# Attention and a dense layer on one core: deeper buffers for the weights' conversion, and the first scores sent in two halves

## The chip, the core and the metric

The kernel runs on one core of a Trainium2 chip. The core has TensorE (matrix products, in the profile PE, its weight loads PEld), VectorE (DVE), ScalarE (ACT), GpSimd (POOL) and SyncE (SP, which here only issues DMAs); they run side by side and wait for one another by semaphores. The time is the device time of one execution in microseconds (us); lower is better. Three runs of the kernel before gave a median of 971.5 us (971.06 to 972.27).

## What is computed

Talking-heads attention over 4 batches, 12 heads, 448 positions and 64 channels, then a gated dense layer over its 1792 rows:

```python
scores = scale * np.matmul(q, k.transpose(0, 1, 3, 2))
scores = np.einsum('bhij,hg->bgij', scores, w_pre)      # mix over heads
attn = softmax(scores)
attn = np.einsum('bhij,hg->bgij', attn, w_post)         # mix over heads again
x = np.matmul(attn, v)                                  # then rows (b, s), columns (h, d): 1792 x 768
h = x @ w_in                                            # w_in 768 x 2048
out = (h * (1 / (1 + np.exp(-h)))) @ w_out              # w_out 2048 x 768
```

The two dense weights come as 64-bit floats and have to be turned into 32-bit ones on the chip.

## The kernel before

**Attention.** Each batch's 448 queries are cut into 4 tiles of 12 or 11 groups of 10 queries, 180 groups in 16 tiles. For a tile, TensorE makes scores head by head (line 277), ScalarE and VectorE copy them to SBUF (`st`, or `first` for tile 0, lines 282 and 284) and a DMA regroups them (line 286): `g` has one partition for each pair of query and head, so that one product mixes the heads. For each group, `mix` (315) multiplies with w_pre, `top` (321) takes the maximum on VectorE, `exp` runs on ScalarE (326), `norm` makes 1/sum on VectorE (331, 332) and scales w_post by it on GpSimd (`wr`, 334), `mix_again` (341) multiplies with it, ScalarE copies the result (`at`, 349). `values` (297) multiplies with v.

**The opening.** Before the loop, tile 0's keys and queries are transposed (`prep_k`, `prep_q`) and its scores made; `banks` and `steps` set the order. All of tile 0's score regrouping has to be in `g` before its first mix. The first four heads of tile 1's scores come here too.

**The loop** (from line 546) takes one group at a time: the mix of group i+3, copies, the maximum, `norm` of i+2, the exp of i+3, then scores, transposes and values that a table `work` gave to this group, then `mix_again` of i. Each engine runs its instructions in the order written.

**The weights' conversion** (`convert`, line 38) is a generator that the loop steps along. A weight block (a job) is two parts; a part takes two groups of the loop. It loads 256 KB into a buffer `cw` (47), VectorE takes the exponent (88), ScalarE shifts it (92), VectorE puts sign and mantissa in (94, 95) and, one part later, joins the low word (64), GpSimd multiplies (67). After two parts GpSimd makes sums (70 to 73) into `ct` and into the block `cg`, and two stores send both to DRAM (57, 58). 42 of 48 jobs run in attention, in the groups of the set `lighter` (which holds every group of the loop up to the last tile); the other 6 run in the dense layers. Buffers: three `cw`, two `cg`, one `ct`. At part k the load of part k+1 is issued:

```python
        if k > 1:
            load(k + 1)
```

into the buffer that part k-2 gave back. A tile's buffers belong to a pool; an instruction that writes one first waits for everything that used it before.

**DMA queues.** Nearly every DMA is issued by SyncE, in the order of the program. A DMA that waits for its data, or for the DMA eight places earlier to land, holds up those behind it.

**After attention** the converted blocks are loaded (`wl`, 485), split in high and low parts and multiplied (501 to 503).

Of the kernel before, what the change touches and what calls it, by code (L numbers as in the profile page):

```python
# [8 lines left out]
F32 = mybir.dt.float32  # L9
F32R = mybir.dt.float32r  # L10
I32 = mybir.dt.int32
# [11 lines left out]
def raw(ap):  # L23

    return ap.bitcast(F32)
# [9 lines left out]
    eng.tensor_sub(out=lo, in0=x, in1=raw(hi))  # L35


def convert(nc, pool, ebias, jobs):

    parts = [(n, i) for n in range(len(jobs)) for i in (1, 0)]  # L40
    loaded, made = [], []

    def load(k):
        if k < len(parts):
            n, i = parts[k]
            ws = pool.tile([128, 2, 256], I32, name="cw", tag="cw", bufs=3)
            nc.sync.dma_start(out=ws, in_=jobs[n][0][:, i])
            loaded.append(ws.rearrange("p q (w t) -> p q w t", t=2))

    for k in range(3):  # L50
        load(k)
    yield

    def store():
        while made:
            dst, g, t = made.pop(0)
            nc.sync.dma_start(out=dst[:, :4], in_=g)
            nc.sync.dma_start(out=dst[:, 4:], in_=t)

    def finish(k, pair, g, e):  # L60
        n, i = parts[k]
        lo, hi = pair[:, :, :, 0], pair[:, :, :, 1]
        m = lo.bitcast(F32)
        nc.vector.scalar_tensor_tensor(  # L64
            out=m, in0=lo.bitcast(U32), scalar=(1 if i else -1) * 2.0 ** -32, in1=hi,
            op0=ALU.mult, op1=ALU.add if i else ALU.subtract)
        nc.gpsimd.tensor_mul(out=e, in0=m, in1=e)  # L67
        if not i:
            t = pool.tile([128, 3, 128], F32, name="ct", tag="ct", bufs=1)
            nc.gpsimd.tensor_add(out=t[:, 0], in0=g[:, 0], in1=g[:, 1])  # L70
            nc.gpsimd.tensor_add(out=t[:, 1], in0=g[:, 0], in1=g[:, 2])
            nc.gpsimd.tensor_add(out=t[:, 2], in0=t[:, 0], in1=g[:, 2])
            nc.gpsimd.tensor_add(out=g[:, 0], in0=t[:, 2], in1=g[:, 3])
            made.append((jobs[n][1], g, t))

    before = None
    for k in range(len(parts)):
        if k > 1:
            load(k + 1)
        pair = loaded.pop(0)  # L80
        hi = pair[:, :, :, 1]
        if k % 2 == 0:
            g = pool.tile([128, 4, 128], F32, name="cg", tag="cg", bufs=2)
        else:
            store()
        half = g[:, 2 * (k % 2):2 * (k % 2) + 2]
        e = half.bitcast(I32)
        nc.vector.tensor_scalar(out=e, in0=hi, scalar1=0x7FF00000, scalar2=None, op0=ALU.bitwise_and)  # L88
        if before:
            finish(*before)  # L90
        yield True
        nc.scalar.activation(out=e, in_=e, func=AF.Relu, scale=8.0, bias=ebias)  # L92
        yield False
        nc.vector.scalar_tensor_tensor(out=e, in0=hi, scalar=-2 ** 31, in1=e, op0=ALU.bitwise_and, op1=ALU.bitwise_or)
        nc.vector.tensor_scalar(out=hi, in0=hi, scalar1=0xFFFFF, scalar2=1 << WEXP, op0=ALU.bitwise_and, op1=ALU.bitwise_or)
        before = k, pair, g, half
        yield
    if before:
        finish(*before)
    yield  # L100
    store()
    yield
# [3 lines left out]
def talking_heads_then_silu_mlp(  # L106
# [11 lines left out]
    nc = tc.nc  # L118
# [4 lines left out]
    R = 10  # L123
# [114 lines left out]
    def load_q(n, hg, queue=nc.sync):  # L238
        b, ti = seq[n]
        t0, m, _ = tiles[ti]  # L240
        qns[n, hg] = nat.tile([TQ, HH, D], F32, name="qn", tag="qn", bufs=2)
        queue.dma_start(out=qns[n, hg][:m], in_=q[b, hg * HH:(hg + 1) * HH, t0:t0 + m, :].rearrange("h p d -> p h d"))

    def prep_q(n, hg):

        t0, m, ng = tiles[seq[n][1]]
        NP = HH // 2
        qh, ql = qs[n, hg] = [q2_p.tile([128, NP, TQ], F32R, name=x, tag=f"{x}{hg}") for x in ("qh", "ql")]
        qn = qns.pop((n, hg))
        pt = bank(banks[0], "pt")  # L250
        for hh in range(NP):
            nc.tensor.transpose(
                pt[:, hh * m:(hh + 1) * m], qn[:m, 2 * hh:2 * hh + 2, :].rearrange("p h d -> p (h d)"), ident[:m, :m])
        src = pt[:, :NP * m].rearrange("p (h g i) -> p h g i", h=NP, i=R)
        hi, lo = (x[:, :, :m].rearrange("p h (i g) -> p h g i", i=R) for x in (qh, ql))

        def take_high():
            nc.scalar.copy(out=hi, in_=src)

        def take_low():  # L260
            nc.vector.tensor_sub(out=lo, in0=src, in1=raw(hi))
        return [(take_high, take_low)]

    def scores(n, h):

        b, ti = seq[n]
        t0, m, ng = tiles[ti]
        if h == 0:
            gs[n] = g_ps[(len(seq) - 1 - n) % 2].tile([GP, 12, S], F32, name="g", tag="g")
        qh, ql = qs[n, h // HH]  # L270
        kh, kl = ks[b, h]
        hh = h % HH // 2
        ps = [bank(banks[0], "pqk") for _ in range(2)]
        for step, (q_, k_) in enumerate(((qh, kh), (ql, kh), (qh, kl))):
            for i in range(2):
                rows = slice(i * D, (i + 1) * D)
                nc.tensor.matmul(ps[i][:m, :S], lhsT=q_[rows, hh, :m], rhs=k_[rows], start=(step == 0), stop=(step == 2))  # L277

        def take(i):
            st = s_p.tile([TQ, S], F32, name="st", tag="s") if n else first_scores[:, h + i]  # L280
            if i:
                nc.vector.tensor_copy(out=st[:m], in_=ps[i][:m, :S])  # L282
            else:
                nc.scalar.copy(out=st[:m], in_=ps[i][:m, :S])  # L284
            queue = nc.scalar if n == 0 and i == 0 and h % 4 == 2 else nc.sync
            queue.dma_start(out=gs[n][h + i:GP:H, :ng, :], in_=st[:m])
        return [(lambda: take(0), None), (None, lambda: take(1))]

    def values(n, h):
# [63 lines left out]
    jobs = [(wi_src[:, f, c], wi_dram[:, :, f * HC + c, :]) for f in range(HF) for c in range(HC)]  # L353
    jobs += [(wo_src[:, c, f], wo_dram[:, :, c * HF + f, :]) for c in range(HC) for f in range(HF)]
    NA = 42
    conv = convert(nc, c_p, ebias, jobs[:NA])

    groups, first = [], []
    for n, (b, ti) in enumerate(seq):
# [46 lines left out]
    lighter = set()  # L406
    for i in range(0, n_last, 10):
        lighter |= set(sorted(range(i, min(i + 10, n_last)), key=lambda i: weight[i - 1] if i else 0.0)[:10])
    lighter |= {n_last - 1, n_last - 2}


    first_scores = a_p.tile([TQ, H, S], F32, name="first", tag="at")
# [11 lines left out]
    steps += [(prep_q, 1, 0)] + [(scores, 1, 2 * h) for h in range(NE)]  # L424
    nk = 6
    weights = load_weights()
    for j, (what, *args) in enumerate(steps):
        banks[:] = [(ps_m, ps_m, ps_p, ps_a)[j % 4]]
        takes = what(*args)
        for take in (x for t in takes for x in t):  # L430
            if take:
                take()
        if what is prep_k and nk < H:
            load_k_pair(0, nk)
            nk += 2
        if j == 5:
            next(weights)
            load_q(1, 0, nc.gpsimd)
        if j == 12:
            load_q(1, 1, nc.gpsimd)  # L440
    banks[:] = [ps_m]
    for _ in weights:
        pass
    for i in range(3):
        at(i).mix()
        at(i).top()
# [337 lines left out]
```

## Time and profile before

| | us |
|---|---|
| median of three runs | 971.5 |
| the profiled execution | 972.25 |
| its span, first to last instruction | 970.5 |
| TensorE busy | 918.2 |
| VectorE busy | 635.6 |
| ScalarE busy | 543.4 |
| GpSimd busy | 453.4 |

An engine that is busy for a large share of the span isn't for that reason the limit at every moment: TensorE's matmuls are pipelined, their ends are modelled, and its busy time stretches where the clock is lower. The granted clock is the share of TensorE's full clock that was given in a stretch; 0.5 is the lower of its two levels. Who waits for whom is inferred from semaphores; an instruction that waits for several is put down to the one that came last.

### The profile page before, as it was taken

Reading aid. Unit: us, or ns where it says so; the run is one execution under the profiler, and the core shown is the slowest. Engines: PE = TensorE matmul, PEld = TensorE weight load, DVE = VectorE, ACT = ScalarE, POOL = GpSimd, SP = SyncE. Lnnn points to the kernel's source line nnn. Section 1 sums busy time; section 2 is a strip of 40 time slices with the busy share of each in tenths; the row PEclk is TensorE's granted clock in tenths of the full one; section 3 lists DMA queues with packets and bytes.
Section 4 is the critical chain, followed back from the end, with each engine's and each line's share of the span. In section 5 each row is a group of like instructions: output and inputs, shape, how many; then the busy total and the mean of one; then the engine's idle time right before and its main releaser. Section 6 shows DMA issues by size and latency. Waiting matters only on the chain.

```text
span 970.5 us, 18406 instructions
## 1 busy us (share of the span) xinstructions
PE 918.2 (95%) x6216; PEld 742.3 (76%) x6216; DVE 635.6 (65%) x1414; ACT 543.4 (56%) x1256; POOL 453.4 (47%) x627
## 2 busy tenths in 40 slices
PE   6789999999899989998999999999999999999997
PEld 4466676667676666665767999889999999889996
DVE  4577676657676757666665069865568977997432
ACT  4466676667576757666667455522368435443242
POOL 1154444444345434444444256895333767784130
PEclk9899999999999989999999999999999999999999
DMA  6677765767667768767563035521122113221134
GB/s 161 171 208 192 198 190 170 209 195 201 186 174 219 192 170 217 193 182 199 166 179 104 1 112 155 148 60 44 55 66 65 55 51 84 66 66 55 47 87 114
DMA packets 166399, 131.18 MB, mean 135 GB/s; under 512 B 50134, under 2 KB 155466, under 8 KB 166306
## 3 DMA queue, kind: packets, MB, share of 16 engines
q1 hardware_dynamic: 164300, 128.66, 48.1%
q10 hardware_dynamic: 1782, 0.99, 0.4%
q8 instruction: 50, 0.82, 0.4%
q0 software_dynamic: 224, 0.35, 0.2%
q14 instruction: 43, 0.35, 0.1%
HBM read 63.74 MB, written 27.53 MB: 94 GB/s over the span
## 4 chain that ended last, share of the span: by engine, by line
PE 66%; DMA 12%; DVE 8%; POOL 5%; issue 4%; ACT 3%; SPq 1%; ACTq 0%; POOLq 0%; DVEq 0%
PE ph L503 12%; PE ph L502 12%; PE ph L501 12%; PE pa L341 9%; PE pp L315 8%; PE po L297 6%; DMA wi_dram<-cg 4%; PE pqk L277 4%; DMA cw<-in_moe_w_out 3%; DVE nm L321 2%; DMA cw<-in_moe_w_in 2%; DVE st L282 2%; POOL wl L491 1%; DMA kn<-in_k 1%; POOL cg L67 1%
## 5 line engine op out<-in xcount | busy, mean ns | idle before, releaser
L341 PEld LDWEIGHTS pa<-wr,e 120*112 120x112 f32 x1440 | 165.4, 178 | 42.7 <-issue 26.4
L491 POOL TENSOR_TENSOR wl<-wl,wh 128x512 fp32r<-128x512 f32 x84 | 122.0, 1462 | 156.0 <-ACT wh L490 151.2
L341 PE MATMUL pa<-wr,e 120*112 120x120 f32 x1440 | 187.7, 274 | 1.6 <-POOL wr L334 0.8
L334 POOL TENSOR_SCALAR wr<-wpost,r 120x120 f32<-120x120 f32 x180 | 78.7, 438 | 215.7 <-DVE r L332 170.4
L315 PE MATMUL pp<-g,wpre 120*120 120x448 f32 x360 | 169.5, 554 | 8.8 <-DMA g<-st 5.1
L503 PE MATMUL ph<-op,wl 128*128 128x448 f32 x462 | 169.2, 366 | 1.6 <-POOL wl L491 1.6
L501 PE MATMUL ph<-op,wh 128*128 128x448 f32 x462 | 170.4, 369 | 0.0
L502 PE MATMUL ph<-op,wh 128*128 128x448 f32 x462 | 168.8, 365 | 0.0
L321 DVE TENSOR_REDUCE nm<-pp 120x1 f32<-120x448 f32 x180 | 111.5, 620 | 83.5 <-PE pp L315 82.7
L326 ACT ACTIVATE e<-pp,nm 120x448 f32<-120x448 f32 x180 | 114.7, 637 | 80.7 <-DVE r L331 47.2
L349 ACT COPY at<-pa 112x480 f32<-112x480 f32 x180 | 102.3, 568 | 48.2 <-PE pa L341 48.1
L67 POOL TENSOR_TENSOR cg<-cw,cg 128x256 f32<-128x256 f32 x96 | 72.4, 755 | 93.1 <-DVE cw L64 93.1
L297 PEld LDWEIGHTS po<-at,v 112*64 112x64 f32 x1536 | 77.0, 140 | 37.4 <-ACT st L284 11.1
L503 PEld LDWEIGHTS ph<-op,wl 128*128 128x128 f32 x462 | 86.8, 188 | 10.1 <-POOL wl L491 3.1
L297 PE MATMUL po<-at,v 112*64 112x110 f32 (+1 forms) x1536 | 87.1, 268 | 6.8 <-ACT st L284 6.7
L501 PEld LDWEIGHTS ph<-op,wh 128*128 128x128 f32 x462 | 86.8, 188 | 6.8
L502 PEld LDWEIGHTS ph<-op,wh 128*128 128x128 f32 x462 | 86.8, 188 | 6.6
L88 DVE TENSOR_SCALAR cg<-cw 128x256 int32<-128x256 int32 x96 | 32.0, 334 | 79.5 <-DMA cw<-in_moe_w_out 26.1
L490 ACT CAST wh<-wl 128x512 fp32r<-128x512 f32 x84 | 51.0, 618 | 46.9 <-DMA wl<-wo_dram 26.3
L92 ACT ACTIVATE cg<-cg,ebias 128x256 int32<-128x256 int32 x96 | 49.1, 512 | 41.3 <-DVE cg L88 41.3
L509 DVE TENSOR_TENSOR op<-x,op 128x448 fp32r<-128x448 f32 x54 | 46.2, 866 | 31.2 <-ACT op L507 17.7
L315 PEld LDWEIGHTS pp<-g,wpre 120*120 120x120 f32 x360 | 53.1, 187 | 13.7 <-ACT e L326 7.1
(107 smaller groups left out, 1612.5 us busy)
## 6 DMA issues: line engine op xcount, KB each, us to landing
g<-st SPq DMA_DIRECT2D x144, 192.5 KB
cw<-in_moe_w_in SPq DMA_DIRECT2D x48, 256.0 KB
cw<-in_moe_w_out SPq DMA_DIRECT2D x48, 256.0 KB
wl<-wi_dram SPq DMA_DIRECT2D x42, 256.0 KB
wl<-wo_dram SPq DMA_DIRECT2D x42, 256.0 KB
g<-st SPq DMA_DIRECT2D x36, 210.0 KB
wi_dram<-cg SPq DMA_DIRECT2D x24, 256.0 KB
wo_dram<-cg SPq DMA_DIRECT2D x24, 256.0 KB
```

What stands on the lines that cost most here:

```text
L67: nc.gpsimd.tensor_mul(out=e, in0=m, in1=e)
L297: nc.tensor.matmul(po[i * D:(i + 1) * D, c * m:(c + 1) * m], lhsT=vs[b, h + 2 * c][:, i, j, :], rhs=ats[n][:, j, h + 2 * c + i, :m], start ...
L315: nc.tensor.matmul(self.p[:GP, :S], lhsT=wpre.rearrange("p i g -> p (i g)"), rhs=gs[self.n][:, self.slot, :], start=True, stop=True)
L321: nc.vector.tensor_reduce(out=self.nm, in_=self.p[:GP, :S], axis=AX.X, op=ALU.max, negate=True)
L326: nc.scalar.activation(out=self.e, in_=self.p[:GP, :S], func=AF.Exp, bias=self.nm, scale=1.0, accum_out=self.s)
L334: nc.gpsimd.tensor_scalar(out=self.wr, in0=wpost.rearrange("p g i -> p (g i)"), scalar1=r, scalar2=1.0, op0=ALU.mult, op1=ALU.mult)
L341: nc.tensor.matmul(self.pa[:JT, j * GP:(j + 1) * GP], lhsT=self.e[:, j * JT:(j + 1) * JT], rhs=self.wr, start=True, stop=True)
L349: nc.scalar.copy(out=ats[self.n][:, :, :, o:o + R], in_=self.src)
L491: nc.gpsimd.tensor_sub(out=wl, in0=raw(wl), in1=raw(wh))
L501: nc.tensor.matmul(p[:, :T], lhsT=wh, rhs=x[:, 0], start=(n == 0), stop=False)
L502: nc.tensor.matmul(p[:, :T], lhsT=wh, rhs=x[:, 1], start=False, stop=False)
L503: nc.tensor.matmul(p[:, :T], lhsT=wl, rhs=x[:, 0], start=False, stop=(n == nk - 1))
```

## The change

The conversion gets five `cw` buffers, three `cg` buffers and, in attention, two `ct` buffers, and loads three parts ahead. It no longer runs in groups 0 to 2. Tile 0's scores are sent to `g` in two halves of its twelve groups: for each head a store of groups 0 to 5 when its scores are copied, and the twelve stores of groups 6 to 11 after the last head; all of them on SyncE, where three of the twelve were on ScalarE. For the halves to be one block of partitions each, the query conversion of tile 0 is written half by half. The weights of the head mix are prepared earlier, and tile 1's second query half is loaded by SyncE behind the 24 stores, no longer by GpSimd.

```diff
--- before.py
+++ after.py
@@ -35,7 +35,7 @@
     eng.tensor_sub(out=lo, in0=x, in1=raw(hi))
 
 
-def convert(nc, pool, ebias, jobs):
+def convert(nc, pool, ebias, jobs, cts=1):
 
     parts = [(n, i) for n in range(len(jobs)) for i in (1, 0)]
     loaded, made = [], []
@@ -43,7 +43,7 @@
     def load(k):
         if k < len(parts):
             n, i = parts[k]
-            ws = pool.tile([128, 2, 256], I32, name="cw", tag="cw", bufs=3)
+            ws = pool.tile([128, 2, 256], I32, name="cw", tag="cw", bufs=5)
             nc.sync.dma_start(out=ws, in_=jobs[n][0][:, i])
             loaded.append(ws.rearrange("p q (w t) -> p q w t", t=2))
 
@@ -66,7 +66,7 @@
             op0=ALU.mult, op1=ALU.add if i else ALU.subtract)
         nc.gpsimd.tensor_mul(out=e, in0=m, in1=e)
         if not i:
-            t = pool.tile([128, 3, 128], F32, name="ct", tag="ct", bufs=1)
+            t = pool.tile([128, 3, 128], F32, name="ct", tag="ct", bufs=cts)
             nc.gpsimd.tensor_add(out=t[:, 0], in0=g[:, 0], in1=g[:, 1])
             nc.gpsimd.tensor_add(out=t[:, 1], in0=g[:, 0], in1=g[:, 2])
             nc.gpsimd.tensor_add(out=t[:, 2], in0=t[:, 0], in1=g[:, 2])
@@ -75,12 +75,11 @@
 
     before = None
     for k in range(len(parts)):
-        if k > 1:
-            load(k + 1)
+        load(k + 3)
         pair = loaded.pop(0)
         hi = pair[:, :, :, 1]
         if k % 2 == 0:
-            g = pool.tile([128, 4, 128], F32, name="cg", tag="cg", bufs=2)
+            g = pool.tile([128, 4, 128], F32, name="cg", tag="cg", bufs=3)
         else:
             store()
         half = g[:, 2 * (k % 2):2 * (k % 2) + 2]
@@ -251,14 +250,19 @@
         for hh in range(NP):
             nc.tensor.transpose(
                 pt[:, hh * m:(hh + 1) * m], qn[:m, 2 * hh:2 * hh + 2, :].rearrange("p h d -> p (h d)"), ident[:m, :m])
-        src = pt[:, :NP * m].rearrange("p (h g i) -> p h g i", h=NP, i=R)
-        hi, lo = (x[:, :, :m].rearrange("p h (i g) -> p h g i", i=R) for x in (qh, ql))
+        src = pt[:, :NP * m].rearrange("p (h g) -> p h g", h=NP)
+        W = 1 if n else 2
+        blocks = [slice(w * m // W, (w + 1) * m // W) for w in range(W)]
+        srcs = [src[:, :, w].rearrange("p h (g i) -> p h g i", i=R) for w in blocks]
+        his, los = ([x[:, :, w].rearrange("p h (i g) -> p h g i", i=R) for w in blocks] for x in (qh, ql))
 
         def take_high():
-            nc.scalar.copy(out=hi, in_=src)
+            for hi, src in zip(his, srcs):
+                nc.scalar.copy(out=hi, in_=src)
 
         def take_low():
-            nc.vector.tensor_sub(out=lo, in0=src, in1=raw(hi))
+            for lo, src, hi in zip(los, srcs, his):
+                nc.vector.tensor_sub(out=lo, in0=src, in1=raw(hi))
         return [(take_high, take_low)]
 
     def scores(n, h):
@@ -282,8 +286,16 @@
                 nc.vector.tensor_copy(out=st[:m], in_=ps[i][:m, :S])
             else:
                 nc.scalar.copy(out=st[:m], in_=ps[i][:m, :S])
-            queue = nc.scalar if n == 0 and i == 0 and h % 4 == 2 else nc.sync
-            queue.dma_start(out=gs[n][h + i:GP:H, :ng, :], in_=st[:m])
+            if n == 0:
+                for w in range(2):
+                    def put_scores(w=w):
+                        nc.sync.dma_start(out=gs[n][h + i:GP:H, 6 * w:6 * w + 6, :], in_=st[60 * w:60 * w + 60])
+                    if w:
+                        second.append(put_scores)
+                    else:
+                        put_scores()
+            else:
+                nc.sync.dma_start(out=gs[n][h + i:GP:H, :ng, :], in_=st[:m])
         return [(lambda: take(0), None), (None, lambda: take(1))]
 
     def values(n, h):
@@ -353,7 +365,7 @@
     jobs = [(wi_src[:, f, c], wi_dram[:, :, f * HC + c, :]) for f in range(HF) for c in range(HC)]
     jobs += [(wo_src[:, c, f], wo_dram[:, :, c * HF + f, :]) for c in range(HC) for f in range(HF)]
     NA = 42
-    conv = convert(nc, c_p, ebias, jobs[:NA])
+    conv = convert(nc, c_p, ebias, jobs[:NA], 2)
 
     groups, first = [], []
     for n, (b, ti) in enumerate(seq):
@@ -406,7 +418,7 @@
     lighter = set()
     for i in range(0, n_last, 10):
         lighter |= set(sorted(range(i, min(i + 10, n_last)), key=lambda i: weight[i - 1] if i else 0.0)[:10])
-    lighter |= {n_last - 1, n_last - 2}
+    lighter = lighter - set(range(3)) | {n_last - 1, n_last - 2}
 
 
     first_scores = a_p.tile([TQ, H, S], F32, name="first", tag="at")
@@ -424,6 +436,8 @@
     steps += [(prep_q, 1, 0)] + [(scores, 1, 2 * h) for h in range(NE)]
     nk = 6
     weights = load_weights()
+    next(weights)
+    second = []
     for j, (what, *args) in enumerate(steps):
         banks[:] = [(ps_m, ps_m, ps_p, ps_a)[j % 4]]
         takes = what(*args)
@@ -433,14 +447,15 @@
         if what is prep_k and nk < H:
             load_k_pair(0, nk)
             nk += 2
-        if j == 5:
-            next(weights)
+        if j == 3:
+            for _ in weights:
+                pass
             load_q(1, 0, nc.gpsimd)
-        if j == 12:
-            load_q(1, 1, nc.gpsimd)
+        if (what, *args) == (scores, 0, H - 2):
+            for put_scores in second:
+                put_scores()
+            load_q(1, 1)
     banks[:] = [ps_m]
-    for _ in weights:
-        pass
     for i in range(3):
         at(i).mix()
         at(i).top()
```

What SyncE issues in the opening, before. `qn` is a query half, `kn` a head's keys, `g<-first` tile 0's regrouping, `g<-st` tile 1's, `cw` the conversion's loads, `v` values:

```order
L242 DMA qn<-in_q 120x6x64
L214 DMA kn<-in_k 112x4x64 x6
L286 DMA g<-first 10x12x448 x9
L286 DMA g<-st 10x11x448 x4
L47 DMA cw<-in_moe_w_in 128x2x256 x3
L218 DMA v_384<-in_v 112x2x256
L218 DMA v_386<-in_v 112x2x256
```

And in the changed kernel, same place:

```order
L241 DMA qn<-in_q 120x6x64
L213 DMA kn<-in_k 112x4x64 x6
L292 DMA g<-first 10x6x448 x24
L241 DMA qn<-in_q 110x6x64
L298 DMA g<-st 10x11x448 x4
L47 DMA cw<-in_moe_w_in 128x2x256 x3
L217 DMA v_400<-in_v 112x2x256
L217 DMA v_402<-in_v 112x2x256
```

Nine whole stores became 24 halves, and a query load of tile 1 stands behind them.

What TensorE does from the first mix on, with its waits, in the changed kernel (`pp` is the mix, `pt` a transpose, `pa` the second mix; DMAHW0 to 7 are the eight semaphores that SyncE's and ScalarE's DMAs take in turn):

```order
L327 MATMUL pp<-g,wpre 120x448 [waits DMAHW4_49,DMAHW3_49,DMAHW5_49,DMAHW2_49,DMAHW6_49,DMAHW1_49,DMAHW7_49,DMAHW0_49,PE_49]
L327 MATMUL pp<-g,wpre 120x448 [waits PE_49]
L327 MATMUL pp<-g,wpre 120x448 [waits Activation_49] x2
L251 MATMUL pt<-ident,qn 128x110 [waits DMAHW6_49]
L251 MATMUL pt<-ident,qn 128x110 x2
L353 MATMUL pa<-wr,e 112x120 [waits Pool_49]
L353 MATMUL pa<-wr,e 112x120 x3
```

TensorE's own order is that of before; the transpose `pt` waited for GpSimd's queue there and now waits for SyncE's load. The mix of group 6 has waits on these semaphores of its own.

VectorE at the start of the last tile, before (`nm` is a group's maximum, `r` its 1/sum, `cg` and `cw` the conversion):

```order
L88 TENSOR_SCALAR cg<-cw 128x256
L64 SCALAR_TENSOR_TENSOR cw<-cw 128x256
L321 TENSOR_REDUCE nm<-pp 120x1
L331 TENSOR_SCALAR r<-s 120x1
L332 RECIPROCAL r<-r 120x1
L94 SCALAR_TENSOR_TENSOR cg<-cw,cg 128x256
L95 TENSOR_SCALAR cw<-cw 128x256
L321 TENSOR_REDUCE nm<-pp 120x1
L331 TENSOR_SCALAR r<-s 120x1
L332 RECIPROCAL r<-r 120x1
L64 SCALAR_TENSOR_TENSOR cw<-cw 128x256
L321 TENSOR_REDUCE nm<-pp 120x1
```

And in the changed kernel:

```order
L93 SCALAR_TENSOR_TENSOR cg<-cw,cg 128x256
L94 TENSOR_SCALAR cw<-cw 128x256
L87 TENSOR_SCALAR cg<-cw 128x256
L64 SCALAR_TENSOR_TENSOR cw<-cw 128x256
L93 SCALAR_TENSOR_TENSOR cg<-cw,cg 128x256
L94 TENSOR_SCALAR cw<-cw 128x256
L64 SCALAR_TENSOR_TENSOR cw<-cw 128x256
L333 TENSOR_REDUCE nm<-pp 120x1
```

The conversion's last part was spread between the groups' maxima and now stands in one block ahead of one.

## Rows read from the trace of the kernel before

**Rows 1.** The page: its span, and TensorE's busy tenths in 40 slices.

```profile
span 970.5 us, 18406 instructions
...
PE   6789999999899989998999999999999999999997
```

**Rows 2.** Windows: busy us and instructions per engine, granted clock, DMA share, GB/s.

```profile
36.00:541.00 505.00, 475.06 (x3971) 342.37 (x3971) 333.02 (x1007) 335.28 (x850) 221.32 (x434) 0.98 0.67 183
265.00:325.00 60.00, 59.05 (x513) 42.61 (x512) 42.61 (x130) 43.00 (x109) 27.66 (x55) 1.00 0.69 193
361.00:404.00 43.00, 41.61 (x352) 29.65 (x351) 29.49 (x87) 29.81 (x75) 17.25 (x35) 1.00 0.75 201
100.00:145.00 45.00, 43.19 (x371) 30.95 (x369) 31.61 (x93) 31.30 (x79) 19.73 (x39) 1.00 0.72 192
...
196.00:206.00 10.00, 7.75 (x59) 5.66 (x57) 5.66 (x19) 5.10 (x13) 4.50 (x9) 0.83 0.62 173
246.00:256.00 10.00, 7.70 (x42) 5.39 (x42) 4.92 (x15) 4.73 (x12) 1.74 (x4) 0.83 0.69 177
346.00:356.00 10.00, 7.78 (x54) 6.33 (x55) 6.40 (x20) 5.81 (x15) 4.69 (x9) 0.66 0.51 147
456.00:466.00 10.00, 7.62 (x62) 6.04 (x59) 4.81 (x15) 4.57 (x12) 4.15 (x8) 0.83 0.69 186
```

**Rows 3.** Who waited for whom, VectorE, 36 to 541: us, times, longest.

```profile
DVE cg L88 <- DMA cw<-in_moe_w_out: 23.8, 10, 4.7
DVE cg L88 <- DMA wi_dram<-cg: 23.6, 13, 3.9
DVE cg L88 <- DMA cw<-in_moe_w_in: 19.1, 11, 3.6
DVE cg L88 <- DMA wo_dram<-cg: 10.0, 5, 4.0
```

**Rows 4.** The chain of waits in order of time: start, us, what.

```profile
26.01 3.71 DMA g<-st
...
79.73 0.74 POOL cg L67
...
80.67 5.31 DMA cw<-in_moe_w_in
...
179.68 4.73 DMA wi_dram<-cg
...
186.99 0.50 PE pt L252 x3
```

**Rows 5.** Timeline of SyncE's issues, 10 to 30: start, us, instructions merged.

```profile
10.97 14.94 SPq L286 DMA_DIRECT2D g<-first  x9
26.01 3.64 SPq L286 DMA_DIRECT2D g<-st  x4
```

**Rows 6.** Line 286, 0 to 36: issue in ns, least/median/most, first and last start.

```profile
L286 SPq DMA_DIRECT2D g<-first x9: 755/756/1537, 11.0 to 25.2; - x9
L286 SPq DMA_DIRECT2D g<-st x4: 755/756/756, 26.0 to 28.9; - x4
```

**Rows 7.** Timeline of VectorE, 14 to 21: the copies of tile 0's scores.

```profile
14.51 0.62 DVE L282 COPY first<-pqk 120x448 f32<-120x448 f32 x1 [0.25 <-PE pqk L277]
...
18.88 1.68 DVE L282 COPY first<-pqk 120x448 f32<-120x448 f32 x3
```

**Rows 8.** DMA issues of tile 1's query halves: count, KB each, us to landing.

```profile
qn<-in_q POOLq DMA_DIRECT2D x2, 165.0 KB, 4.6
```

**Rows 9.** Timeline of TensorE, 29 to 37: first mix, transposes of the second query half.

```profile
29.95 4.42 PE L315 MATMUL pp<-g,wpre 120*120 120x448 f32 x6 [5.10 <-DMA g<-st]
...
35.59 0.45 PE L252 MATMUL pt<-ident,qn 110*128 110x110 f32 x3
```

**Rows 10.** Timeline of TensorE, 521 to 524: the second mixes of two groups.

```profile
521.38 0.98 PE L341 MATMUL pa<-wr,e 120*112 120x120 f32 x8
...
522.95 0.98 PE L341 MATMUL pa<-wr,e 120*112 120x120 f32 x8
```

## Prediction

> **What bounds the kernel now.** I read the page's span and slices first, then a table of windows, then who waited for whom on VectorE, then the chain of waits, then the opening engine by engine. The profiled execution took 972.25 us, 970.5 of them between its first and last instruction [rows 1], 0.75 above the median of 971.5. TensorE is in the nines from slice 20 to the last but one [rows 1]: the dense layers are TensorE's own, so what happens in attention moves the end one for one.
>
> Attention's loop runs from 36 to 541 us. TensorE is busy 475.06 of these 505 us, so 29.9 us are idle [rows 2]. Four windows of 10 us show what the idle time drags along: their granted clock is 0.83, 0.83, 0.66 and 0.83, that is 1.7 + 1.7 + 3.4 + 1.7 = 8.5 us lost at the lower of the clock's two levels, each time just after TensorE stood still [rows 2]. Idle and clock together are 38.4 us.
>
> Who starts it: in the loop VectorE stands still at line 88, the first instruction of a part of the weights' conversion, 23.8 + 23.6 + 19.1 + 10.0 = 76.5 us in 39 waits, all ended by a DMA: the load `cw` in 21 of them, the store of `cg` in 18 [rows 3]. The chain shows both kinds. At 79.73 GpSimd multiplies an old part, its buffer is free, the load starts at 80.67, takes 5.31 and ends on VectorE's line 88 [rows 4]. A store issued at 179.68 takes 4.73; at 186.99 TensorE comes out of a stall at a transpose [rows 4]. VectorE works in order: behind line 88 stand the maximum `nm`, the reciprocal and score copies, so exp, wr and PSUM banks come late. It is a ring: load k+1 starts when part k-2 is finished, which is barely ahead of its use.
>
> **The change part by part.** *Five load buffers, loads three parts ahead.* The buffer of load k+3 is the one part k-2 gave back, as before, but the use is now three parts away. A part takes two groups, about 5.6 us (505 over 180 groups), so the load has some 16 us for what took 5.31. The 21 load waits should go. *Three result buffers, two for `ct`.* A `cg` buffer is wanted again three parts after its store is issued, not one: 16 us for 4.73. The 18 store waits go. No instruction is added in this part.
>
> What the 76.5 us of waits are worth on TensorE I take from windows. Three steadier ones (265 to 325, 361 to 404, 100 to 145) are 148 us long with 0.95 + 1.39 + 1.81 = 4.15 us idle and full clock [rows 2]. At that rate (2.8%) the loop would idle 14.2 us instead of 29.9, and 8.5 of clock come back: 24.3 us. A second way: in these windows TensorE issues 513 + 352 + 371 = 1236 matmul records in 148 us, 8.35 per us, against 3971 in 505, 7.86 per us; at 8.35 the loop takes 475.5, which is 29.5 less [rows 2]. The first is low, since these windows hold such waits themselves. Ends: 38.4 (all idle and clock) and 10 (the loads come in time, but ScalarE and VectorE, busy 335 and 333 of 505, keep TensorE waiting as they do in the window 361 to 404, where it issues 8.19 per us and a steady share of small waits is left). I take **27**.
>
> *First scores in halves.* Before, nine stores of 210 KB left SyncE between 10.97 and 25.91 [rows 5] and three left ScalarE. Now SyncE issues 24 halves, twelve as the scores come, twelve after them, and then the load of the second query half of tile 1, which was on GpSimd's queue long before. Does an issue cost half for half the bytes? The nearest rows: 0.756 us for 120 rows (210 KB), 0.756 for 110 rows (192.5 KB) [rows 6]: no dependence on size. So I price a half at the same, 0.85 with the gap to the next one. The third and fourth score blocks are copied at 14.51 + 0.62 = 15.13 [rows 7]; from there SyncE is the limit: the 12th half is issued at 15.13 + 9 x 0.85 = 22.8. With 3.71 to land [rows 4] the first mix starts at about 26.7 instead of 29.95 [rows 9]: 3.2 earlier. But three mixes and one more behind it is the transpose of that query half, at 35.59 before, 5.64 after the first mix [rows 9]; TensorE can't pass it. The 24th half is issued at 15.13 + 21 x 0.85 = 33.0, the query at 33.8; with the 4.6 of its kind [rows 8] it lands at 38.4. TensorE waits there, and the transpose is 2.8 late. What is queued behind: the rest of TensorE's program. What waits on SyncE: four stores of tile 1's scores and the first `cw` loads, not needed until group 3. Ends: 2 (landing in 3.7) and 6 (the second standstill brings the lower clock again, as it did at 346 [rows 2]); if an issue cost 0.43, the copies that end at 18.88 + 1.68 [rows 7] would be the limit, the query would land at 20.56 + 13 x 0.43 + 4.6 = 30.8, and the transpose would be 4.8 early. I take **+3**.
>
> ScalarE loses three issues, the two query conversions become four shorter instructions, `wpre` and `wpost` move earlier: all of it lies beside SyncE's queue, at 0; without that cover it could give back up to three issues of 0.76 [rows 6] or cost as much.
>
> *Tail.* Conversion skips groups 0 to 2, so its last part runs in one go at the last tile's start: seven VectorE instructions ahead of a `nm`. It is at most like the longest wait at line 88, 4.7 [rows 3]; TensorE has two groups of 1.57 (521.38 to 522.95) in hand there [rows 10]. I take **+1** of 0 to 4.7. In the dense layers the six parts left also load earlier; TensorE is full there: 0.
>
> Sum: 972.25 - 27 + 3 + 1 = 949.25 for an execution like the profiled one, 948.5 at the median.
>
> **Rivals.**
> 1. *Cheaper issues.* If half a store costs half an issue, the opening is -4.8 instead of +3: 940.7. For it: the rows hold only whole stores, and a half has 60 rows instead of 120. Against it: equal cost at 110 and 120 rows [rows 6]. The Trainium skill (DMA: Bandwidth & Descriptors, Issuing engines are not separate DMA queues) stands on this rival's side: issuing from several engines saves only the sequencer's issue time, which it calls usually small beside the transfer. Taken at its word, moving three stores and a load onto SyncE would cost nothing, the opening would keep its 3.2, and the time would be 942.3. The trace doesn't bear out the "small" here: 0.756 of issue stands beside 3.71 of transfer, and 24 of them are in one queue.
> 2. *The wait changes hands.* Line 88 no longer stops VectorE, but the loop's next limit is close: the window 361 to 404 has few such waits and still runs at 8.19. Then the loop gives 10: 965.5. Against it: the window 265 to 325 at 8.55, with part of these waits still in it.
> 3. *Everything comes back*: 38.4 in the loop: 937.1. For it: 500 us of attention with hardly another DMA wait on VectorE; against it: idle time is left in every window of the loop.
> 4. *Slower: the query behind 24 stores.* One mechanism at one place: TensorE's transpose of tile 1's second query half waits for a load that SyncE issues last. Price 6 with the lower clock, 10 if each issue takes 0.91 (3.64 for four, [rows 5]) and the landing is a slow one. It decides if the loop gives less than that, that is if TensorE caught up after each VectorE stall anyway: 972.25 + 6 - 0.75 = 977.5. Against it: idle time of 29.9 with the clock falling four times is not caught up.
> 5. *The halves don't part*: if the first mix still waited for all 24, it would start at 33 + 3.7 instead of 29.95, 7 late: 952.5 at the median.
>
> **Chances.** Forecast 0.47, rival 1 0.17, rival 2 0.18, rival 3 0.08, rival 4 0.06, rival 5 0.04. The range 935 to 966 holds all but rival 4 and the tails. 0.2% of 971.5, which is 1.9 us and about what a measurement of this kernel tells from none, makes faster 0.90, the same 0.04, slower 0.06.
>
> **What would show it.** In the changed profile VectorE's line 87 (88 before) has next to no DMA wait in the loop; TensorE's idle there is below 20 us and the granted clock holds; stores of `first` on SyncE take about 0.75 each; the first mix is at 26 to 27 us and the transpose of the second query half at 37 to 39. Wrong would be: line 87 still waiting, for a load or for GpSimd; or the waits gone and TensorE's idle the same, with exp or wr as its releaser; or issues of half a microsecond.

## The result, and the profile after

The changed kernel took 946.5 us in the median of four runs (944.59 to 948.09), the kernel before in the same rounds 971.88; the ratio is 0.9725, 95% interval 0.9681 to 0.977. Predicted were 948.5 and 935 to 966. The profiled execution took 947.88, its span 946.1. Its span and TensorE's tenths on the page answer to [rows 1]: the eights of the loop are gone but one, slice 21 (473 to 497 us, the start of the last tile), and slice 2, in the opening, is a six where it was a seven.

```profile
span 946.1 us, 18430 instructions
...
PE   6699999999999999999989999999999999999997
```

The first and the last four windows of [rows 2], in the changed kernel, with the loop cut where it now ends:

```profile
36.00:514.00 478.00, 466.10 (x3931) 337.61 (x3932) 334.17 (x1004) 334.54 (x846) 223.91 (x431) 0.99 0.72 198
...
196.00:206.00 10.00, 10.00 (x88) 7.37 (x87) 7.80 (x23) 7.36 (x19) 5.29 (x10) 1.00 0.69 184
246.00:256.00 10.00, 9.67 (x91) 6.92 (x88) 6.75 (x23) 6.79 (x20) 4.68 (x9) 1.00 0.74 196
346.00:356.00 10.00, 9.61 (x82) 6.70 (x82) 7.36 (x20) 7.00 (x18) 4.77 (x9) 1.00 0.81 209
456.00:466.00 10.00, 10.00 (x105) 7.55 (x100) 7.66 (x24) 6.83 (x20) 5.10 (x11) 1.00 0.59 176
```

Idle time of TensorE in the loop is 478 - 466.10 = 11.9 us instead of 29.9, and the four windows that stood at clocks of 0.66 to 0.83 are at 1.00. (The windows hold later groups than before: at 206 us the kernel is 8 us ahead of its old self, at 466 it is 27 ahead.) Who waited on VectorE in that stretch [rows 3] (us, times, longest); the waits below this line are of 0.6 us and less:

```profile
DVE nm L333 <- PE pp L327: 129.0, 115, 7.9
```

Of the 76.5 us at the conversion's first instruction (line 87 now) nothing is left; VectorE waits for TensorE's mix. TensorE's longest group of waits before (37 to 538), for a score copy on ScalarE, and now (40.6 to 514), for VectorE's `r`:

```profile
PE pt L252 <- ACT st L284: 11.3, 9, 2.6
...
PE pqk L281 <- DVE r L343: 4.1, 12, 0.4
```

The opening is the other side. SyncE's issues, the answer to [rows 5]:

```profile
11.01 24.04 SPq L292 DMA_DIRECT2D g<-first  x24
35.16 0.44 SPq L241 DMA_DIRECT2D qn<-in_q  x1
35.70 3.34 SPq L298 DMA_DIRECT2D g<-st  x4
39.10 2.05 SPq L47 DMA_DIRECT2D cw<-in_moe_w_in  x3
```

The durations of one of line 292 in ns, least, median and most [rows 6]:

```profile
L292 SPq DMA_DIRECT2D g<-first x24: 748/748/1013, 11.0 to 34.3; - x24
```

And TensorE's timeline with the first mix and the transpose [rows 9]:

```profile
27.46 4.32 PE L327 MATMUL pp<-g,wpre 120*120 120x448 f32 x6 [2.58 <-DMA g<-first]
...
38.17 0.81 PE L251 MATMUL pt<-ident,qn 110*128 110x110 f32 x3 [4.91 <-DMA qn<-in_q]
```

A half costs SyncE the 0.75 us of a whole. The first mix is 2.5 earlier than before, the transpose 2.6 later, behind the query load, as in the prediction. In the opening the chain of waits now runs through the second halves on SyncE into that load, where before it ran through a store of tile 1's scores [rows 4]:

```profile
33.51 0.75 SPq L292
34.30 0.75 SPq L292
...
35.16 2.98 DMA qn<-in_q
38.17 0.81 PE pt L251 x3
```

Where the 24.4 us went is seen on one copy per group, `at` (line 349 before, 361 after). ScalarE's timeline: start, us, instruction; the first group, group 158 (the first of tile 14, counting from 0) and the last, before:

```profile
37.08 0.56 ACT L349 COPY at<-pa 112x480 f32<-112x480 f32 x1
...
489.94 0.57 ACT L349 COPY at<-pa 112x480 f32<-112x480 f32 x1 [0.53 <-PE pa L341]
...
537.61 0.57 ACT L349 COPY at<-pa 112x480 f32<-112x480 f32 x1 [2.11 <-PE pa L341]
```

and after:

```profile
40.62 0.57 ACT L361 COPY at<-pa 112x480 f32<-112x480 f32 x1 [5.94 <-PE pa L353]
...
462.92 0.57 ACT L361 COPY at<-pa 112x480 f32<-112x480 f32 x1 [0.54 <-PE pa L353]
...
513.64 0.57 ACT L361 COPY at<-pa 112x480 f32<-112x480 f32 x1 [2.11 <-PE pa L353]
```

The third column is the first experiment's, below:

| stretch | before | after | deep_only |
|---|---|---|---|
| start to the first group | 37.1 | 40.6 | 36.6 |
| first group to group 158 | 452.9 | 422.3 | 420.0 |
| group 158 to the last | 47.7 | 50.7 | 46.1 |
| rest, the dense layers | 432.9 | 432.5 | 433.5 |

So the change is +3.5 in the opening, -30.6 in the loop, +3.0 in the last two tiles. What the loop's 30.6 are made of, the window from the first group to group 158 shows, before and after:

```profile
37.08:489.94 452.86, 424.83 (x3501) 303.29 (x3500) 305.43 (x920) 301.51 (x766) 197.69 (x393) 0.98 0.70 190
...
40.62:462.92 422.30, 415.64 (x3501) 298.66 (x3501) 306.15 (x916) 302.36 (x762) 200.14 (x387) 1.00 0.76 208
```

TensorE's idle time falls from 28.0 to 6.7 us, by 21.4, and its busy time for the same 3501 records by 9.2, with the granted clock up from 0.98 to 1.00.

### The profile page after: what moved, and what is told of

It reads as the page before. It is cut to its first block, busy times and chain, and to the rows that moved or that the text cites. A ratio compares the mean times of both kernels' runs of the same rounds, so it can differ in the third digit from the quotient of the medians.

```text
span 946.1 us, 18430 instructions
## 1 busy us (share of the span) xinstructions
PE 911.9 (96%) x6216; PEld 740.0 (78%) x6216; DVE 638.6 (68%) x1416; ACT 544.9 (58%) x1258; POOL 457.8 (48%) x626
## 4 chain that ended last, share of the span: by engine, by line
PE 81%; DVE 5%; DMA 5%; POOL 4%; issue 2%; ACT 1%; SPq 1%; POOLq 0%; ACTq 0%; DVEq 0%
PE pa L353 16%; PE pp L327 13%; PE ph L518 12%; PE ph L517 12%; PE ph L516 12%; PE po L309 8%; PE pqk L281 6%; DMA qn<-in_q 2%; POOL wl L506 2%; PE pt L226 1%; DMA kn<-in_k 1%; DMA cw<-in_moe_w_out 1%; SPq L292 1%; DVE nm L333 1%; PE ptt L721 1%
## 5 line engine op out<-in xcount | busy, mean ns | idle before, releaser
L346 POOL TENSOR_SCALAR wr<-wpost,r 120x120 f32<-120x120 f32 x180 | 87.4, 486 | 271.0 <-DVE r L344 228.7
L309 PEld LDWEIGHTS po<-at,v 112*64 112x64 f32 x1536 | 74.2, 137 | 29.7 <-ACT e L338 12.5
L309 PE MATMUL po<-at,v 112*64 112x110 f32 (+1 forms) x1536 | 84.1, 263 | 0.0
L281 PEld LDWEIGHTS pqk<-kh,qh 64*110 64x110 f32 (+1 forms) x192 | 19.8, 178 | 41.9 <-DVE cw L64 9.2
L286 DVE COPY st<-pqk 110x448 f32<-110x448 f32 (+1 forms) x90 | 51.6, 615 | 0.8 <-PE pqk L281 0.8
```

What stands on the lines that cost most here:

```text
L309: nc.tensor.matmul(po[i * D:(i + 1) * D, c * m:(c + 1) * m], lhsT=vs[b, h + 2 * c][:, i, j, :], rhs=ats[n][:, j, h + 2 * c + i, :m], start ...
L346: nc.gpsimd.tensor_scalar(out=self.wr, in0=wpost.rearrange("p g i -> p (g i)"), scalar1=r, scalar2=1.0, op0=ALU.mult, op1=ALU.mult)
```

## The experiments

Ratios are to the kernel before, which ran in the same rounds (medians 970.6 to 971.9), with their 95% intervals.

**deep_only.** Of the change only the convert function and its call:

```diff
-            ws = pool.tile([128, 2, 256], I32, name="cw", tag="cw", bufs=3)
+            ws = pool.tile([128, 2, 256], I32, name="cw", tag="cw", bufs=5)
-        if k > 1:
-            load(k + 1)
+        load(k + 3)
```

and three `cg`, two `ct`.

> The kernel before with only the conversion's buffers deeper (five cw, three cg, two ct, loads three parts ahead); opening, query load and the groups that convert are those of before. Theory (the loop gives it all, the opening costs 3.5 and the tail 1 to 3): 972 less 27 to 31, that is 941 to 945, at or a little below the changed kernel's 946.5. Rival (halves or the later start of the conversion carry part of the gain): 950 or more.

Measured: 938.0 us, 0.9648 (0.9624 to 0.9673): better than expected, and better than the whole change, whose interval it doesn't touch. The last column of the table: opening as before, loop -32.9, last tiles -1.5. TensorE is idle 467 - 459.55 = 7.5 us in the loop, at full clock:

```profile
36.00:503.00 467.00, 459.55 (x3925) 333.15 (x3924) 335.34 (x1006) 334.55 (x848) 224.87 (x432) 1.00 0.72 198
```

So the buffers carry more than the whole gain, and the rest of the change costs some 8.5 us on top of them.

**loads_only and results_only.** Each ring alone: the lines of the diff above; or, with these left as before, `bufs=3` for `cg` and 2 for `ct`. 

> The kernel before with the load side alone: five cw buffers, loads three parts ahead; two cg, one ct as before. By waits in proportion: 21 of the 39 waits at line 88, 42.9 of 76.5 us, so some 56% of 29: about 956. Rival (one ring: with loads early, the store of cg, two parts away, becomes the limit and takes the waits over): the store waits grow from 33.6 us to well over 40 and the time is 962 or more.

> The kernel before with the result side alone: three cg, two ct buffers; three cw and loads one part ahead as before. By waits in proportion: 33.6 of 76.5 us, some 44% of 29: about 959. Rival (one ring): the load waits take over, 60 us or more of them at line 88, and the time is 966 or more.

Measured: 959.92, 0.9861 (0.9823 to 0.9899), and 963.3, 0.9916 (0.9886 to 0.9946), each between its two expectations. VectorE's waits, 36 to 530, with early loads:

```profile
DVE cg L87 <- DMA wi_dram<-cg: 25.8, 13, 4.1
DVE cg L87 <- DMA wo_dram<-cg: 18.6, 10, 4.0
```

and with more result buffers:

```profile
DVE cg L88 <- DMA cw<-in_moe_w_out: 37.1, 16, 5.2
DVE cg L88 <- DMA cw<-in_moe_w_in: 36.4, 21, 3.5
```

The side that was mended is clean; on the other the waits grow, from 33.6 to 44.4 us for stores and from 42.9 to 73.5 for loads [rows 3]. By the medians the two alone give 11 + 8 = 19 us, together 33. That is the rivals' mechanism: a part that is freed of one wait reaches the other earlier.

**two_ahead.** deep_only with four `cw` and this load:

```diff
-        load(k + 3)
+        if k:
+            load(k + 2)
```

> deep_only (938.0) with four cw buffers and loads two parts ahead instead of five and three. Theory (the ring needs only more time than a load's 5 to 9 us to land; two parts are some 11 us): 937 to 940, no waits of over 1 us at line 87. Rival (landings of 8 to 9 us behind bunches of stores eat the margin): line 87 waits for loads again, 20 us or more of them, 942 to 948.

Measured: 937.2, 0.9641 (0.9606 to 0.9675), one wait of 0.6 us at line 88. The theory holds: one part ahead is too little, two are enough, the fifth buffer buys nothing that can be measured.

**halves_only.** The changed kernel with the buffers of before:

```diff
-            ws = pool.tile([128, 2, 256], I32, name="cw", tag="cw", bufs=5)
+            ws = pool.tile([128, 2, 256], I32, name="cw", tag="cw", bufs=3)
-        load(k + 3)
+        if k > 1:
+            load(k + 1)
```

and two `cg`, one `ct`.

> The changed kernel with the conversion's buffers and load distance of before (three cw, two cg, one ct, load one part ahead): halves, query load behind them and the later start of the conversion remain. Theory (all but the deeper buffers costs time; against deep_only it cost 8.5): 975 to 981, slower than before. Rival (in a loop that stops at line 88 anyway, the opening's 4 us are absorbed): 969 to 973.

Measured: 972.29, 1.0009 (0.9988 to 1.0031): the rival. Alone the other half of the change costs next to nothing, beside the deeper buffers 8.5 us. By the copy `at` its opening is 2.4 later than before (39.47), and the loop, still with waits at line 88, gives 1.2 of it back. Its last two tiles take 48.1, 0.4 more than before. So a loop that waits anyway hides a late start in part, as far as one profile shows it; in the changed kernel, whose loop is full, the start that is 4.0 behind deep_only's is 6.3 behind at group 158.

**query_first.** In the changed kernel:

```diff
         if (what, *args) == (scores, 0, H - 2):
+            load_q(1, 1)
             for put_scores in second:
                 put_scores()
-            load_q(1, 1)
```

> The changed kernel with one move: tile 1's second query half is loaded by SyncE ahead of the twelve second halves instead of behind them. Theory (the opening's loss is that load): it is issued about 9 us earlier, the transposes run where the program has them, 5.6 after the first mix, at about 33.1 instead of 38.2, and the second stretch at the lower clock (37.6 to 44.5 in the changed kernel) goes or shrinks; the time falls by 4 to 6.5, to 940 to 943. Rival (the loss comes from the halves or from group 6's mix waiting for late second halves, one issue later still here): the transposes move, but the time stays within 1.5 of 946.5.

Measured: 946.34, 0.9755 (0.9724 to 0.9785): no change. The transposes came as the theory has it, but a wait of the same size followed. TensorE's timeline:

```profile
32.38 0.45 PE L251 MATMUL pt<-ident,qn 110*128 110x110 f32 x3
...
48.73 0.78 PE L251 MATMUL pt<-ident,qn 110*128 110x110 f32 x3 [5.40 <-DMA qn<-in_q]
```

Now tile 2's first query half is late. The first `at` is at 33.86, 2.8 ahead of deep_only; that of group 12, at 70.76, is 5.4 behind it (65.33). The theory's place was right and its claim that the loss was that load alone was wrong.

**both_first.** Both query loads go ahead of the second halves, and the loop's own load of tile 2's first half goes:

```diff
-                if n > 1:
+                if n > 1 and (n, hg) != (2, 0):
...
-        if (what, *args) == (scores, 0, H - 2):
+        if (what, *args) == (prep_q, 1, 0):
+            load_q(1, 1)
+            load_q(2, 0)
             for put_scores in second:
                 put_scores()
-            load_q(1, 1)
```

> The changed kernel with the load of tile 1's second query half and that of tile 2's first ahead of the twelve second halves; in query_first the wait for the first went (transposes at 32.4) and one for the second came (5.4 us at 48.7). Theory (these two loads are all that the queue of halves made late): first mix near 26.7, no wait of over 1 us for a query up to 60 us, so 5 to 6 less than query_first: 939 to 942. Rival (24 issues of 0.75 and the stores behind them fill queue and transfer engines until some 60 us, so the next load or the stores of tile 1's scores are late instead): 944 to 947.

Measured: 946.13, 0.9741 (0.9707 to 0.9774): the rival again. No transpose waits for a query, and TensorE stands still a few groups later:

```profile
53.25 1.94 PE L353 MATMUL pa<-wr,e 120*112 120x120 f32 x8 [6.08 <-POOL wr L346]
```

The row names GpSimd; its `wr` waits for VectorE's reciprocal, and VectorE stands at a score copy whose buffer is still being stored:

```profile
49.60 0.62 DVE L286 COPY st<-pqk 110x448 f32<-110x448 f32 x1 [4.40 <-DMA g<-st]
51.75 0.62 DVE L286 COPY st<-pqk 110x448 f32<-110x448 f32 x1 [1.52 <-DMA g<-st]
```

In the chain of waits that store, issued at 43.84, takes 7.89 us, where such a store took 3.71 before [rows 4]. Three kernels, three waits (a query, the next query, a store), each of 4.9 to 6.1 us: something behind them is late, not one transfer. The windows 22 to 36 and 36 to 60 show it (granted clock, DMA share and GB/s are the last three columns). deep_only:

```profile
22.00:36.00 14.00, 7.66 (x29) 3.63 (x30) 5.59 (x15) 3.97 (x9) 0.73 (x2) 0.76 0.73 216
36.00:60.00 24.00, 21.99 (x144) 14.77 (x143) 18.41 (x57) 18.11 (x44) 11.33 (x22) 1.00 0.79 199
```

The changed kernel:

```profile
22.00:36.00 14.00, 7.06 (x20) 2.65 (x20) 5.36 (x14) 4.75 (x12) 1.09 (x3) 0.88 0.47 134
36.00:60.00 24.00, 21.77 (x124) 15.00 (x125) 12.64 (x40) 13.56 (x32) 4.68 (x10) 0.86 0.82 218
```

both_first:

```profile
22.00:36.00 14.00, 9.98 (x38) 4.71 (x38) 5.57 (x15) 5.52 (x13) 1.10 (x3) 0.76 0.52 146
36.00:60.00 24.00, 17.52 (x98) 12.49 (x100) 11.57 (x38) 11.97 (x30) 5.33 (x12) 0.86 0.83 204
```

While SyncE issues halves, one of 105 KB per 0.79 us, the transfer engines are half idle: 105 KB in 0.79 us are 136 GB/s, and the changed kernel's window shows 134. In deep_only, where whole stores and then `cw` and `v` loads left in this window, their share is 0.73. What was not moved by 36 us is moved after it, and whichever transfer the program needs first is late.

**second_split.** both_first with the odd heads' second halves issued by GpSimd (which sends them as the scores come, from 11.72 to 21.97, the rest as before):

```diff
-                    def put_scores(w=w):
-                        nc.sync.dma_start(out=gs[n][h + i:GP:H, 6 * w:6 * w + 6, :], in_=st[60 * w:60 * w + 60])
+                    def put_scores(w=w, queue=nc.gpsimd if w and i else nc.sync):
+                        queue.dma_start(out=gs[n][h + i:GP:H, 6 * w:6 * w + 6, :], in_=st[60 * w:60 * w + 60])
```

> both_first with six of the twelve second halves (the odd heads') issued by GpSimd instead of SyncE; bytes and their destinations are the same. Theory (a half costs SyncE the 0.75 us of a whole, so from 22 to 36 us the transfer engines are only half used, 0.52 against 0.73 in deep_only, and the backlog fills them from 40 to 60): SyncE is through some 4.7 us earlier, the DMA share of 22 to 36 rises to 0.6 or more, the 6.1 us wait at 53 shrinks to 2 or less, and the time falls to 941 to 943. Rival (what is late is the sum of the bytes, whoever issues them): share and wait stay, 945 to 948.

Measured: 943.85, 0.9705 (0.9667 to 0.9743), between the two expectations; the interval still overlaps that of both_first, so the times alone don't part the two. The profile's opening is plainer: the share of 22 to 36 rises to 0.61, the 6.1 us wait is gone, one of 2.1 is left, and group 12's `at` is at 66.39, against 70.41 in both_first and 65.33 in deep_only.

```profile
22.00:36.00 14.00, 9.91 (x39) 4.76 (x37) 5.31 (x14) 4.90 (x12) 1.09 (x3) 0.76 0.61 174
...
56.27 1.25 PE L327 MATMUL pp<-g,wpre 120*120 120x448 f32 x2 [2.07 <-DMA v<-in_v]
```

With the same bytes and six issues moved, 4.0 of 5.1 us in the opening came back, so that SyncE's issues were the cause of most of it. The run also starts those six halves earlier (11.72 to 21.97 instead of after 25.83); it doesn't tell that from SyncE's shorter queue. The gain doesn't reach the end of this profiled execution (946.54): its last two tiles take 50.6 us where both_first's take 48.7, and its dense layers some 4 us longer; why is not shown. The Trainium skill (DMA: Bandwidth & Descriptors, Issuing engines are not separate DMA queues) says that issuing from several engines saves only the time of the issue, usually small beside the transfer. Issue time is what was saved here, but it was not small: 0.75 us for 105 KB, where a whole store took 3.71 to land [rows 4].

**skip_only.** deep_only plus the later start of the conversion:

```diff
-    lighter |= {n_last - 1, n_last - 2}
+    lighter = lighter - set(range(3)) | {n_last - 1, n_last - 2}
```

> Deeper buffers alone (deep_only, 938.0), plus one part of the change: the conversion does not run in groups 0 to 2, so that its last part runs in one block at the last tile's start. Theory (the tail's and a part of the loop's loss in the changed kernel come from this shift: against deep_only the changed kernel loses 1.3 at group 54, 0.7 at group 110 and 4.6 in groups 165 to 170): 941 to 945, with those steps in the same groups. Rival (they are late echoes of the opening's queue, not of the shift): 937 to 939.

Measured: 940.08, 0.9674 (0.9644 to 0.9704), a little under the theory's range and above the rival's; the interval overlaps deep_only's, so it is the profile that tells. By the copy `at` it is level with deep_only to within 0.8 us up to group 164, and 3.6 behind at the last. TensorE's row is that of the changed kernel, here skip_only:

```profile
475.49 0.98 PE L314 MATMUL pp<-g,wpre 120*120 120x448 f32 x2 [2.08 <-DMA wo_dram<-cg]
```

and the changed kernel:

```profile
481.07 1.52 PE L327 MATMUL pp<-g,wpre 120*120 120x448 f32 x2 [1.92 <-DMA wo_dram<-cg]
482.38 1.80 PE L353 MATMUL pa<-wr,e 120*112 120x120 f32 x8
...
495.76 1.07 PE L353 MATMUL pa<-wr,e 120*112 120x120 f32 x8 [0.48 <-POOL wr L346]
```

So the tail's loss is the shift's. The other kernels bear it out: from group 158 to the last group the five with deep buffers whose conversion starts at group 3 (this one, the changed one, query_first, both_first, second_split) take 48.3 to 50.7 us, the five where it starts at group 0 (deep_only, two_ahead, three_queues and the two last_halves) 46.1 to 46.2. The 1.52 and 1.80 show the lower clock after the wait in the changed kernel (0.83 from 480 to 490); in skip_only the clock stayed at 1.00. The conversion's last block, which the prediction priced, stands in the 0.48 alone. The rows name `cg`, but a mix reads only `g`, and in query_first the row of the same mix names the stores into `g`:

```profile
480.67 0.98 PE L327 MATMUL pp<-g,wpre 120*120 120x448 f32 x2 [1.22 <-DMA g<-st]
```

By the program it waits for the last stores of tile 15's scores, which SyncE issues in the changed kernel from 473.44 on behind a `cw` load, a `cg` and a `ct`:

```profile
471.77 0.44 SPq L47 DMA_DIRECT2D cw<-in_moe_w_out  x1
472.31 0.41 SPq L57 DMA_DIRECT2D wo_dram<-cg  x1
472.77 0.58 SPq L58 DMA_DIRECT2D wo_dram<-ct  x1
473.44 3.14 SPq L298 DMA_DIRECT2D g<-st  x3
```

In deep_only the conversion is three groups further there. That these DMAs are what delays the stores is argued; no run took them away alone. The steps of 1.3 at group 54 and 0.7 at group 110 were expected here too: the second is there (0.6), the first is not.

**three_queues.** deep_only with three of SyncE's nine whole stores on GpSimd:

```diff
+            if n == 0 and h % 4 == 0 and i == 1:
+                queue = nc.gpsimd
```

> Deeper buffers alone (deep_only, 938.0) with whole stores of the first scores, three of the nine of SyncE moved to GpSimd: six on SyncE, three on ScalarE, three on GpSimd. Theory (the first mix waits for SyncE's issues): six issues fewer than nine, so SyncE ends some 2.3 earlier, first mix at 27 to 27.5 instead of 29.6, 935 to 936.5. Rival (the stores land one per 1.2 to 1.4 us in deep_only whoever issues them, the transfer is the limit): first mix at 28.5 or later, 937 to 938.5, or worse if GpSimd's issues are slow.

Measured: 939.72, 0.9668 (0.9634 to 0.9701): not better, and its profiled execution has the first mix at 31.42, waiting 5.11 for `wpre`. GpSimd issued the second query load only at 29.40 (11.85 in deep_only), behind its three stores, and `blk`, from which VectorE makes `wpre`, stands behind that load (the last of the stores left at 23.1; what held the load after it the profile doesn't show):

```profile
31.04 0.28 DVE L201 TENSOR_TENSOR wpre<-blk,wrep 120x120 f32<-120x120 f32 x1 [4.03 <-POOL blk L198]
```

So it doesn't tell issue from transfer.

**last_halves and last_halves_w.** deep_only with halves for heads 6 to 11 alone, the second halves behind the `cw` loads; the second kernel also prepares the weights early, as the changed one.

```diff
+            if n == 0 and h >= HH:
+                def put_scores(w):
+                    (nc.sync if w else queue).dma_start(
+                        out=gs[n][h + i:GP:H, 6 * w:6 * w + 6, :], in_=st[60 * w:60 * w + 60])
+                put_scores(0)
+                second.append(put_scores)
...
+    for put_scores in second:
+        put_scores(1)
```

> deep_only (938.0) with halves for the last six heads alone: as many stores before the first mix as in deep_only (nine on SyncE, three on ScalarE), six of them half as large, and the six second halves behind the cw loads. Theory (in deep_only the last stores land one per 1.2 us, limited by transfer, not by issue): the first mix starts about 3 earlier, at 26 to 27.5, and the second halves land before group 6 needs them; 934.5 to 936.5. Rival (six more issues of 0.75 push tile 2's query and tile 1's scores back, as in the changed kernel): a wait of 2 us or more between 40 and 60, 938 to 941.

> last_halves (937.1) with the weights of the head mix prepared at the start of the opening, as in the changed kernel; there the first mix waited 0.98 for wpre after its last half had landed at 26.02. Theory: first mix at about 26.5 instead of 27.45, the time 935.5 to 936.8, below both kernels and below deep_only. Rival (the next wait, for exp or the query, takes the microsecond back): 937 to 938.

Measured: 937.09, 0.9637 (0.9605 to 0.9668), and 937.16, 0.9633 (0.9609 to 0.9657). The mix starts as expected, in last_halves

```profile
27.45 6.34 PE L326 MATMUL pp<-g,wpre 120*120 120x448 f32 x8 [0.98 <-DVE wpre L201]
```

and in last_halves_w

```profile
26.37 2.99 PE L326 MATMUL pp<-g,wpre 120*120 120x448 f32 x4 [0.34 <-DMA g<-first]
...
48.01 1.07 PE L352 MATMUL pa<-wr,e 120*112 120x120 f32 x8 [1.76 <-POOL wr L345]
```

yet neither can be told from deep_only: the first lies between its two expectations, the second in its rival's. deep_only's first mix is at 29.60; 2 to 3 us less are worth one at most (group 12 is 0.9 and 0.6 ahead of deep_only's): the groups behind it wait again before 60 us. In last_halves the transfer engines' share from 22 to 36 is 0.61, as in second_split, so that share alone doesn't tell a late queue. The plain deeper buffers are as good as anything that was run here, 8 to 9 us below the changed kernel.

## Why the prediction came out right, and where its steps were off

- *Line 88's waits go, both kinds.* Right, and no rival's wait took their place.
- *Worth 27 in the loop.* Too small: 30.6 in the changed kernel, 32.9 with the buffers alone. Of its first estimate's terms, 15.7 of idle time and 8.5 of clock, the clock was near (9.2) and the idle time was sized too low (21.4). The rate from the steadier windows left in waits of the same kind, as the text said; the second estimate, 29.5 by matmuls per us, was the nearer one, and rival 3, with all idle and clock back (38.4), was a little nearer to deep_only than the forecast. The low end of 10, for small waits that would remain when the loads come in time, was far off: deep_only's TensorE is idle for 7.5 us in the whole loop.
- *A half costs the issue of a whole, 0.756.* Right: 0.748. The 24th half left at 34.3 (33.0 predicted), the query at 35.16 (33.8), the transpose ran at 38.17 (38.4), the first mix at 27.46 (26.7; its own terms, 22.8 and 3.71, add up to 26.5). That the transpose came within 0.2 is luck: the query left 1.4 later than predicted and landed in 2.98 instead of 4.6. The issue times rule out rivals 1 and 5: issues are not cheaper, and the first mix, which ran before the 24th half left, did not wait for all 24.
- *The opening costs 3.* Measured 3.5 at the first group. The mechanism held where it was put, but it was too narrow: rival 4's "one mechanism at one place" is a whole queue that is late, as query_first and both_first showed when the loss moved to the next transfer. Against deep_only it is 4.0 at the first group, 4.6 at group 12.
- *The tail costs 1.* Measured 3.0, against deep_only 4.6. The step that failed is the mechanism: not the conversion's block ahead of a maximum, but the wait of the last tile's first mix and, in the changed kernel, the lower clock after it. The prediction looked only at VectorE's order there, not at the stores on SyncE.
- *The sum.* 24.4 us were gained between the two profiled executions, 23 predicted. Two errors stand against each other: the loop gave about 4 more, the opening and the tail took about 2.5 more. That 948.5 lies 2.0 from 946.5 is in part luck.

## What to carry to other kernels

When a buffer ring makes an engine wait, deepen both of its ends at once: each end alone gave a third or a quarter of the gain, since the other took the waits over. Cutting a transfer in two to have its first half earlier pays for its issues twice; if the issuing queue is already the limit, everything behind it moves back, and taking the load that is waited for out of the queue only names the next one. Test a change of several parts by its parts: here one part gave more than the whole.

## What had not been expected

- Without the buffers the rest of the change was free (1.0009), with them it cost 8.5 us: the two parts' effects don't add.
- What an issue costs SyncE does not go with the bytes: a `cw` load of 256 KB took 0.44 us, a half of 105 KB 0.75.
- In the changed kernel a wait of 1.92 us on TensorE cost nearly as much again by the clock (0.17 of the 10 us from 480 to 490): the same eight products took 1.80 us after it, and 0.98 at full clock [rows 10]. In skip_only a wait of 2.08 us at the same mix did not: the granted clock stayed at 1.00 from 470 to 490. What makes the difference is not shown.
